# A fused attention and MLP kernel: a changed prologue (homes for x tiles, tile 5's transpose, the order of late loads, V by head group, statistics of tile 3)

## The chip, the cores and the metric

One core of a Trainium2 chip runs the kernel. TensorE (PE in the profile) does matmuls, VectorE (DVE), ScalarE (ACT) and GpSimd (POOL) work elementwise, and SyncE (SP) issues every DMA, in one queue. The metric is the device time of one execution in microseconds; the median of three runs is given.

## The reference

A layer norm of x feeds both an attention block and an MLP; the result gates and is added to x. 2048 rows, 1024 columns, 32 heads of 32, hidden width 3584, bf16.

```python
xn = layernorm(x)
q, k, v = heads(xn @ wqkv)                     # 32 heads of 32
s = (softmax(q @ k.T * 32**-0.5) @ v) @ wo     # over 2048 keys
y = layernorm(xn)
b = gelu(y @ w1 + b1) @ w2 + b2                # 1024 -> 3584 -> 1024
out = x + s * silu(b)
```

## The kernel before, in words

The work is cut in 16 tiles of 128 rows of x. A tile is loaded, its mean and variance are taken, it is normalised to bf16 (`normalize`, line 748) and transposed ("turned") into `xnT`, so that the 1024 columns lie on the partitions. Tiles 0 to 3 are turned on TensorE (`tr_item`, 726) and copied from PSUM by ScalarE (737); tiles 4 to 15 are turned by a DMA (752). The statistics of tile 1 come from two ScalarE passes with accumulators (769); all others from VectorE's two `bn_stats` passes and an aggregate (785, 787). The inverse root is a power on GpSimd (794).

From the turned tiles come the queries and keys of head group 0 in blocks of 256 rows (two tiles): `q_item` and `k_item` (706, 716). VectorE copies queries out of PSUM (712), ScalarE copies keys (722). "K2" below is the keys of tiles 4 and 5. `v_item` (677) makes the values of two head groups at once, two tiles at a time, with a right operand of 256 columns.

Eight head groups of four heads follow one another. For a head group and a block of 256 queries, a *unit* takes 256 keys: one step of eight matmuls writes scores to four of six PSUM banks (line 846), and two ScalarE exponentials of 1024 columns (855) turn them into probabilities. Then matmuls with V (612) accumulate the outputs in one of two further banks, and sums of probabilities come from VectorE adds (`tree`, `tree1`; 872, 886, 1209) and a matmul with ones. In the first head group the order of units is written out by hand (`order0`, 1123): two query blocks run side by side, so that keys are used as they come, and a third is mixed in. There are 504 such units and eight of half width at the end.

The MLP (`w1_item`, `w2_item`), the projections of the following head groups (`proj`) and the output projection fill TensorE between the scores. Weights stream through rings of buffers.

Nothing of this order is decided on the chip. `_Plan` holds all operations with assumed costs, priorities and dependences, and runs a list schedule when the program is built: it fixes the order of each engine's instructions, and puts semaphore waits where an operation needs another engine's result. Each engine then runs its list in order. TensorE work sits in queues named `tr`, `pro`, `q0`, `v0`, `proj`, `mlp`, `w2`, `wo`; an item has a position, a due unit, and `hold`, the unit before which it may not start. Where TensorE would be idle early, the plan inserts dummy matmuls with the identity ("fillers", 668).

x tiles share ten buffers inside `hT`, so tiles 10 to 15 are loaded when an earlier tile is normalised (782). `wv` is loaded right after tile 9.

Of the kernel before, what the change touches and what calls it, by code (L numbers as in the profile page):

```python
# [32 lines left out]
class _Plan:  # L33
# [59 lines left out]
    def run(self):  # L93
# [152 lines left out]
        def pe_step(t):  # L246
# [214 lines left out]
def bass_recurrent_scan__mha_block__mixer_channel_mlp__prompt_kernel(  # L461
# [17 lines left out]
    EPS = 1e-5  # L479
# [13 lines left out]
    with ExitStack() as st:  # L493
# [125 lines left out]

        XS = lambda t: ("xst", t % NXS)  # L620

# [3 lines left out]
        def load_x(t, extra=()):  # L625
            dma(f"x{t}", lambda e: e.dma_start(xst[t % NXS], x2[t * 128:(t + 1) * 128, :]), 262144, [], [XS(t)],
                rate=390.0, prio=2, occ=500, lat=2450, extra=extra)
# [9 lines left out]

        def load_v(pr):
            src = A_wqkv[:, 2 * D + pr * 256: 2 * D + (pr + 1) * 256].rearrange("(c p) n -> p c n", p=128)
            dma("wv", lambda e: e.dma_start(wv[:], src), 524288, [], [("wv",)], prio=2, rate=200.0)  # L640

# [35 lines left out]
        def v_item(pr, n, kind, pos=0.0):  # L677
# [14 lines left out]
            return it  # L692

        def qk_item(hg, which, tq, wi, pos):
            it = _Item("proj", pos)
            sl = hg % 2
            for dc in range(DC):
                def fn(e, b, dc=dc):
                    return mm(e, bank(b), wqk[wi][:, dc, :], xnT[:, dc, tq * 512:(tq + 1) * 512], dc == 0, dc == DC - 1)
                chunk(it, fn, Q512, [("xnT", 4 * tq + k, dc) for k in range(4)] + [("wqk", wi)])  # L700
            nm = "Q" if which == 0 else "K"
            dve(lambda e: e.tensor_copy(QKT[sl][:, which, tq * 512:(tq + 1) * 512], bank(it.bank)), c_ps(512), [],  # L702
                [(nm, sl, 2 * tq), (nm, sl, 2 * tq + 1)], 0, it)
            return it
# [11 lines left out]
        def k_item(n):  # L716
            it = _Item("pro", 0.01 * n)
            for dc in range(DC):
                def fn(e, b, dc=dc):
                    return mm(e, bank(b, 0, 256), wqk[wk0][:, dc, :], xnT[:, dc, n * 256:(n + 1) * 256], dc == 0, dc == DC - 1)  # L720
                chunk(it, fn, Q256, [("xnT", 2 * n, dc), ("xnT", 2 * n + 1, dc), ("wqk", wk0)])
            act(lambda e: e.activation(QKT[0][:, 1, n * 256:(n + 1) * 256], bank(it.bank, 0, 256), ACT.Copy), c_act(256), [],
                [("K", 0, n)], -1, it)
            return it

        def tr_item(t):
            it = _Item("pro", t - 10.0)
            it.bank = [2, 3, 4, 5][t]
            tk = ("S", it.bank // 2, it.bank % 2)

# [16 lines left out]
        def normalize(t, rs):  # L747
            first[t] = dve(lambda e: e.tensor_scalar(xnb[t % 4], xst[t % NXS], mv[:, t, 0:1], lnp[:, t, 1:2],  # L748
                                          op0=ALU.subtract, op1=ALU.mult), c_b4(1024) + 118,
                [XS(t), ("mv", t), rs], [("xnb", t % 4)], 1)  # L750
# [12 lines left out]

        for n in range(NPR):
            groups = [(2 * n,), (2 * n + 1,)] if n < 2 else [(2 * n, 2 * n + 1)]
            for ts in groups:
                if ts == (AT,):
                    for k, f, sc in ((0, ACT.Copy, 1.0 / D), (1, ACT.Square, D ** -0.5)):
                        act(lambda e, k=k, f=f, sc=sc: e.activation(
                            fl3(PA[0])[:, k * 1024:(k + 1) * 1024], xst[AT], f, scale=sc, accum_out=mv[:, AT, k:k + 1]),  # L770
                            c_acts(1024) + 93, [XS(AT)], [("st", AT, k)], 1)
                    dve(lambda e: e.tensor_tensor(lnp[:, AT:AT + 1, 2], mv[:, AT:AT + 1, 0], mv[:, AT:AT + 1, 0], op=ALU.mult), 65,
                        [("st", AT, 0)], [("s2",)], 0.95)
                    dve(lambda e: e.scalar_tensor_tensor(lnp[:, AT:AT + 1, 0], mv[:, AT:AT + 1, 1], EPS, lnp[:, AT:AT + 1, 2], op0=ALU.add,
                                                         op1=ALU.subtract), 65,
                        [("st", AT, 1), ("s2",)], [("ve", AT)], 0.95)
                    dve(lambda e: e.tensor_tensor(mv[:, AT:AT + 1, 1], mv[:, AT:AT + 1, 1], lnp[:, AT:AT + 1, 2], op=ALU.subtract), 65,
                        [("st", AT, 1), ("s2",)], [("mv", AT)], 1.1)
                for t in ts:
                    if t == AT:  # L780
                        continue
                    if t >= NXS:
                        load_x(t, [first[2 * n - 5]])
                    for c in range(2):
                        dve(lambda e, t=t, c=c: e.bn_stats(stats[:, t, c, :], xst[t % NXS][:, c * 512:(c + 1) * 512]),  # L785
                            605, [XS(t)], [("st", t, c)], 1.2)
# [3 lines left out]
                rs = ("rs", lo)  # L790
                if ts != (AT,):
                    dve(lambda e, lo=lo, hi=hi: e.tensor_scalar_add(lnp[:, lo:hi, 0], mv[:, lo:hi, 1], EPS), 80,
# [5 lines left out]
            if n < NTR // 2:  # L798
                plan.dense["tr"] += [tr_item(2 * n), tr_item(2 * n + 1)]
            if n < NG0:  # L800
                pro_q.append(q_item(n))
            pro_q.append(k_item(n))
            pro_q.sort(key=lambda it: it.pos)
# [12 lines left out]
        pool(lambda e: e.tensor_tensor(lnp[:, :, 2], mv[:, :, 1], lnp[:, :, 1], op=ALU.mult), 250,  # L816
             rss + [("mv", t) for t in range(NT)], [("s2",)], 2)
        pool(lambda e: e.tensor_tensor(lnp[:, :, 2], lnp[:, :, 2], lnp[:, :, 1], op=ALU.mult), 250, [("s2",)], [("s2",)], 2)
# [146 lines left out]
        def proj(hg, w):  # L965
            wk = load_qk(hg, 1, [first[9]] if hg == 1 else ())
            wq = load_qk(hg, 0)
# [4 lines left out]
            if hg % 2 == 0:  # L972
                lst += [(8 + 5 * n, "v", n) for n in range(NPR)]
            for pos, kind, t in sorted(lst):
                pos += 64 * w
                if kind == "v":
                    it = v_item(hg // 2, t, "proj", pos)
# [142 lines left out]


        pvs = [_Item("pv") for _ in range(NG0)]
        order0 = [(0, 0), (0, 1), (1, 0), (1, 1), (0, 2), (1, 2), (2, 0), (2, 1)]
# [75 lines left out]
        def tree1(g, us):  # L1199
            pr, tok = PR[g % 2], ("PR", g % 2)  # L1200
            for k in range(4):
# [5 lines left out]
                for m in range(2):  # L1207
                    pi = us[2 * k + m][2]
                    dve(lambda e, d=d, m=m, pi=pi: e.tensor_tensor(d[:, m], Pt[pi][:, :, 0, :], Pt[pi][:, :, 1, :], op=ALU.add),
                        c_b16(1024), [("P", pi, h) for h in range(2)], [dt], 3.2, None, [first[NT - 1]])  # L1210
                if k:
                    dve(lambda e, d=d: e.tensor_tensor(fl3(pr), fl3(pr), fl3(d), op=ALU.add), c_b16(2048), [dt, tok], [tok], 3.2)

# [252 lines left out]
```

## Time and profile before

| | us |
|---|---|
| median of three runs (1034.75 to 1036.66) | 1036.16 |
| the profiled execution | 1036.81 |
| its span, first to last instruction | 1035.0 |
| ScalarE busy in it | 1015.9 |
| TensorE busy | 994.5 |
| VectorE busy | 955.7 |

The profile is of one execution. Busy time is the union of an engine's instructions; the end of a matmul is modelled, so a busy TensorE is not TensorE at its peak. A row of the timeline has the start in the span, the length, engine, line, operation, output and input with shapes and a count, and in brackets the idle time of the engine just before and what ended it. The granted TensorE clock was 0.997 over the span. Lines in rows of before are lines of the kernel before.

### The profile page before, as it was taken

How to read it: one execution, taken by the hardware profiler on the slowest of the kernel's cores; microseconds unless marked ns; L12 is line 12 of the kernel's file. 1: busy time of each engine (PE TensorE's matmuls, PEld its weight loads, DVE VectorE, ACT ScalarE, POOL GpSimd, SP SyncE). 2: the span in 40 equal slices, each digit the busy share in tenths (PEclk: the TensorE clock that was granted, in tenths of full speed). 3: DMA queues.
4: the chain of work that ended last, by engine and by line, in shares of the span. 5: the costliest groups of instructions: out<-in, count | busy, mean ns of one | idle time of the engine just before them, and what ended most of it. 6: DMA issues, size and time to landing. Idle time of an engine off the chain costs nothing.

```text
span 1035.0 us, 31625 instructions
## 1 busy us (share of the span) xinstructions
PE 994.5 (96%) x14148; PEld 633.3 (61%) x14217; DVE 955.7 (92%) x1343; ACT 1015.9 (98%) x1093; POOL 12.2 (1%) x21
## 2 busy tenths in 40 slices
PE   8999999999999999999999999999999999999996
PEld 6656566666766566666665666666656665654433
DVE  7899999899799999997899999998999889978896
ACT  7999999999999999999999999999999999999996
POOL 2200000000000000000000000000000000000000
PEclk9999999999999999999999999999999999999998
DMA  7967756545766657446457575565365762963321
GB/s 204 171 155 212 192 151 188 166 114 153 205 182 143 177 163 221 120 133 190 136 147 196 149 224 164 149 181 160 84 165 161 208 177 70 294 209 121 121 84 53
DMA packets 318199, 167.99 MB, mean 162 GB/s; under 512 B 56688, under 2 KB 306032, under 8 KB 318064
## 3 DMA queue, kind: packets, MB, share of 16 engines
q1 hardware_dynamic: 318064, 165.98, 58.1%
q8 instruction: 111, 1.82, 0.7%
q14 instruction: 24, 0.20, 0.1%
HBM read 146.55 MB, written 12.06 MB: 153 GB/s over the span
## 4 chain that ended last, share of the span: by engine, by line
ACT 84%; PE 9%; DMA 3%; DVE 2%; issue 0%; SPq 0%; POOL 0%; DVEq 0%; another core or an unknown queue 0%
ACT P L855 78%; PE ps L617 6%; ACT ut L1040 4%; DMA w2r<-in_B_w_dram 2%; PE ps L846 2%; PE ps L612 1%; ACT gw L1067 1%; ACT P L1157 1%; DVE stats L785 1%; DMA xnT<-gw 0%; DMA hT<-in_A_x_dram 0%; DVE gw L748 0%; DVE PA L872 0%; DVE hT L1391 0%; ACT w2r L855 0%
## 5 line engine op out<-in xcount | busy, mean ns | idle before, releaser
L855 ACT ACTIVATE P<-ps 128x1024 bf16<-128x1024 f32 x988 | 923.6, 1238 | 2.9 <-PE ps L846 2.8
L872 DVE TENSOR_TENSOR PA<-P 128x2048 bf16<-128x2048 bf16 x173 | 209.5, 1215 | 33.5 <-ACT P L855 32.4
L617 PE MATMUL ps<-yT,w1r 128*128 128x256 bf16 x1792 | 228.2, 273 | 0.8 <-DVE QKT L702 0.5
L617 PE MATMUL ps<-w2r,hT 128*128 128x256 bf16 x1792 | 223.7, 273 | 4.0 <-DMA w2r<-in_B_w_dram 2.6
L846 PE MATMUL ps<-QKT 32*128 32x256 bf16 x4032 | 200.2, 273 | 12.9 <-ACT P L855 9.3
L886 DVE TENSOR_TENSOR PR<-PR,PA 128x2048 bf16<-128x2048 bf16 x173 | 209.4, 1211 | 1.3
L617 PEld LDWEIGHTS ps<-yT,w1r 128*128 128x128 bf16 x1792 | 163.6, 98 | 54.8 <-issue 30.2
L617 PEld LDWEIGHTS ps<-w2r,hT 128*128 128x128 bf16 x1792 | 163.3, 98 | 54.6 <-issue 30.8
L846 PEld LDWEIGHTS ps<-QKT 32*128 32x128 bf16 x4032 | 59.8, 92 | 142.1 <-ACT P L855 135.3
L612 PE MATMUL ps<-P,V 128*32 128x256 bf16 (+1 forms) x4080 | 136.8, 272 | 0.3 <-issue 0.3
L617 PE MATMUL ps<-xnT,wqk 128*128 128x512 bf16 (+1 forms) x507 | 118.7, 360 | 7.2 <-issue 2.0
L612 PEld LDWEIGHTS ps<-P,V 128*32 128x32 bf16 x4080 | 95.8, 96 | 31.3 <-issue 22.5
L617 PE MATMUL ps<-wv,xnT 128*128 128x256 bf16 (+1 forms) x575 | 85.8, 285 | 0.9 <-DVE QKT L702 0.7
L617 PEld LDWEIGHTS ps<-xnT,wqk 128*128 128x128 bf16 x560 | 49.3, 98 | 53.7 <-issue 15.6
L1023 DVE TENSOR_TENSOR hT<-ps,b1T 128x512 bf16<-128x512 f32 x112 | 76.4, 682 | 1.8 <-PE ps L617 1.1
L872 DVE TENSOR_TENSOR PR<-P 128x2048 bf16<-128x2048 bf16 x60 | 72.6, 1210 | 1.0 <-ACT P L855 0.8
L617 PEld LDWEIGHTS ps<-wv,xnT 128*128 128x128 bf16 x576 | 53.0, 98 | 22.2 <-issue 9.3
L1040 ACT ACTIVATE ut<-ut 128x2048 bf16<-128x2048 bf16 (+1 forms) x33 | 62.1, 1883 | 0.0
L941 DVE STREAM_TRANSPOSE nt<-ps 128x256 f32<-128x256 f32 x63 | 27.8, 442 | 14.9 <-PE ps L612 14.8
L702 DVE CAST QKT<-ps 128x512 bf16<-128x512 f32 x58 | 39.6, 683 | 1.8 <-PE ps L617 1.4
L1037 DVE TENSOR_TENSOR ut<-hT 128x2048 bf16<-128x2048 bf16 (+1 forms) x33 | 34.7, 1052 | 0.1
L1042 DVE TENSOR_TENSOR hT<-ut,hT 128x2048 bf16<-128x2048 bf16 (+1 forms) x33 | 34.6, 1050 | 0.0
(107 smaller groups left out, 581.3 us busy)
## 6 DMA issues: line engine op xcount, KB each, us to landing
w1r<-in_B_w_dram SPq DMA_DIRECT2D x112, 512.0 KB, 4.5
w2r<-in_B_w_dram SPq DMA_DIRECT2D x128, 448.0 KB, 4.6
hT<-in_A_x_dram SPq DMA_DIRECT2D x20, 256.0 KB, 3.8
wqk<-in_A_wqkv_dram SPq DMA_DIRECT2D x16, 256.0 KB, 4.3
yst<-in_A_x_dram SPq DMA_DIRECT2D x16, 256.0 KB, 4.7
g_scratch<-gw SPq DMA_DIRECT2D x32, 128.0 KB, 3.8
o_scratch<-ot SPq DMA_DIRECT2D x56, 64.0 KB, 3.6
xnT<-o_scratch SPq DMA_DIRECT2D x7, 512.0 KB, 7.2
```

What stands on the lines that cost most here:

```text
L612: ins = e.matmul(dst(j), lhsT=lhsT(j), rhs=rhs(j), start=start, stop=stop, tile_position=(0, 32 * j), skip_group_check=True)
L617: return e.matmul(dst, lhsT=lhsT, rhs=rhs, start=start, stop=stop, skip_group_check=True)
L702: dve(lambda e: e.tensor_copy(QKT[sl][:, which, tq * 512:(tq + 1) * 512], bank(it.bank)), c_ps(512), [], [(nm, sl, 2 * tq), (nm, sl, 2 * t ...
L846: ins = e.matmul(bank(b0[j], kk * 256, (kk + 1) * 256), lhsT=QKT[sl][32 * j:32 * j + 32, 1, kb * 128:(kb + 1) * 128], rhs=QKT[sl][32 * j:3 ...
L855: x = act(lambda e, h=h: e.activation(Pt[pi][:, 2 * h:2 * h + 2].rearrange("p j k q -> p (j k q)"), ps[:, pr[h] * 1024:(pr[h] + 1) * 1024] ...
L872: return dve(lambda e: e.tensor_tensor(dst[:].rearrange("p u j q -> p (u j) q"), src[:].rearrange("p u j k q -> p (u j) k q")[:, :, 0, :], ...
L886: return dve(lambda e: e.tensor_tensor(fl3(pr), fl3(pr), fl3(PA[i]), op=ALU.add), c_b16(2048), [("PA", i), tok], [tok], 3.2)
L941: dve(lambda e: e.transpose(nt_t[:], bank(pv.bank, 256, 512)), c_ps(256) + 120, [], [("nt",)], prio, pv)
L1023: w1_ev[p] = dve(lambda e: e.tensor_tensor(hT[:, hs], bank(it.bank).rearrange("p (k t) -> p k t", k=2), b1T[:, 2 * pi:2 * pi + 2].unsqueez ...
L1037: dve(lambda e: e.tensor_tensor(u_, x_, x_, op=ALU.mult), c_b16(n), hs_, [("ut", ui)], gp)
L1040: act(lambda e: e.activation(u_, u_, ACT.Tanh, scale=GC), c_acts(n), [("ut", ui)], [("ut", ui)], ga)
L1042: dve(lambda e: e.tensor_tensor(x_, u_, x_, op=ALU.mult), c_b16(n), [("ut", ui)] + hs_, hs_, gp)
```

## The change

- Sixteen homes for the sixteen x tiles: ten in `hT` as before, four in the buffers `PR` (later used for sums of probabilities) and two in `yst` (the MLP's input tiles). A tile's load no longer waits for a buffer. Tiles 10 and 11 are issued directly behind tile 9; tiles 12 to 15 wait for the normalisation of tile 4, and `wv` is issued between tiles 13 and 14, instead of directly behind tile 9.
- Tile 5 is turned on TensorE and copied by ScalarE. The plan may put a waiting transpose between the matmuls of an open item.
- The statistics of tile 3, like those of tile 1, are taken by ScalarE.
- The first queries and keys (tiles 0 and 1) become one item, `qk_first`: 128 columns per matmul, tile 0 first, then tile 1 in two halves. K1 is likewise done tile by tile.
- Keys 3 to 7 of head group 0 are copied by VectorE instead of ScalarE.
- V of head group 0 is made by four items of four tiles with 128 columns (`v_half`); V of head group 1 the same way, later, among the projections.
- The adds of `tree1` get priority 2.3 instead of 3.2 (lower goes first), and the plan assumes longer landing times for the DMA turns of tiles 4, 6 and 7.

```diff
+            tq, th = self.dense["tr"], heads["tr"]
+            if use is None and S["do"] is not None and th < len(tq) and tq[th].chunks[0].left == 0 and tq[th].chunks[0].ready <= t:
+                heads["tr"] += 1
+                tq[th].k = 1
+                S["mode"] = "d"
+                commit(tq[th].chunks[0], t)
+                return
...
-        NTR, NWARM, NG0, AT = 4, 8, 3, 1
+        TRP = (5,)
+        PN = ()
+        NTR, NWARM, NG0, AT = 4, 8, 3, (1, 3)
...
+        for i in range(2):
+            pr_flat = PR[i][:].rearrange("p u j q -> p (u j q)")
+            xst += [pr_flat[:, 0:1024], pr_flat[:, 1024:2048]]
+        xst += [yst_t[i][:] for i in range(2)]
...
-        for t in range(4, NXS):
+        for t in range(NTR, 12):
             load_x(t)
-        load_v(0)
...
+        def v_half(h, m, kind, pos=0.0):
+            it = _Item(kind, pos)
+            for t4 in range(4):
+                for dc in range(DC):
+                    def fn(e, b, t4=t4, dc=dc):
+                        tb = 4 * m + t4
+                        return mm(e, bank(b, t4 * 128, (t4 + 1) * 128), xnT[:, dc, tb * 128:tb * 128 + 128],
+                                  wv[:, dc, h * 128:(h + 1) * 128], dc == 0 and t4 == 0, dc == DC - 1)
+                    chunk(it, fn, Q128, [("xnT", 4 * m + t4, dc), ("wv",)])
+            a = V_SLOTS[0][h]
+            dve(lambda e: e.tensor_copy(V[:, a, 4 * m:4 * m + 4, :], bank(it.bank).rearrange("p (t n) -> p t n", t=4)),
+                c_ps(512), [], [("V", a, 2 * m), ("V", a, 2 * m + 1)], 0, it)
             return it
...
         def k_item(n):
             it = _Item("pro", 0.01 * n)
-            for dc in range(DC):
-                def fn(e, b, dc=dc):
-                    return mm(e, bank(b, 0, 256), wqk[wk0][:, dc, :], xnT[:, dc, n * 256:(n + 1) * 256], dc == 0, dc == DC - 1)
-                chunk(it, fn, Q256, [("xnT", 2 * n, dc), ("xnT", 2 * n + 1, dc), ("wqk", wk0)])
+            for lo, w in ((0, 128), (128, 128)) if n < 2 else ((0, 256),):
+                for dc in range(DC):
...
+            if n >= 3:
+                dve(lambda e: e.tensor_copy(QKT[0][:, 1, n * 256:(n + 1) * 256], bank(it.bank, 0, 256)), c_ps(256), [],
+                    [("K", 0, n)], -1, it)
+                return it
...
+        def qk_first():
+            it = _Item("pro", -0.001)
+            for lo, d0, d1 in ((0, 0, 8), (128, 0, 4), (128, 4, 8)):
+                for k, wi in ((0, wq0), (1, wk0)):
...
         def tr_item(t):
-            it = _Item("pro", t - 10.0)
-            it.bank = [2, 3, 4, 5][t]
+            it = _Item("pro", t - 10.0 if t < NTR else 0.019 + 0.0001 * t)
...
-            if t >= NTR:
+            if t >= NTR and t not in TRP:
                 dma(f"tr{t}", lambda e: e.dma_start_transpose(xnT[:, :, t * 128:(t + 1) * 128], xnb[t % 4]), 262144,
-                    [("xnb", t % 4)], [("xnT", t, c) for c in range(DC)], prio=0, rate=300.0, occ=1300, lat=1000)
+                    [("xnb", t % 4)], [("xnT", t, c) for c in range(DC)], prio=0, rate=300.0, occ=1300, lat={4: 2800, 6: 2400, 7: 2000}.get(t, 1000))
...
         for n in range(NPR):
+            if n == 6:
+                for t in range(12, NT):
+                    load_x(t, [first[4]])
+                    if t == 13:
+                        load_v(0, [first[4]])
...
-                if ts == (AT,):
+                if ts[0] in AT:
...
-                    if t >= NXS:
-                        load_x(t, [first[2 * n - 5]])
...
+            pro_q += [tr_item(t) for t in (2 * n, 2 * n + 1) if t in TRP]
+            if n == 0:
+                pro_q.append(qk_first())
...
-        for n in range(NPR):
-            plan.dense["v0"].append(v_item(0, n, "pro", 0.2 + 0.01 * n))
-            plan.dense["v0"][-1].hold = 6 + 1 * n
+        for n in range(NPR // 2):
+            plan.dense["v0"].append(v_half(0, n, "pro", 0.2 + 0.01 * n))
+            plan.dense["v0"][-1].hold = 6 + 2 * n
...
-            wk = load_qk(hg, 1, [first[9]] if hg == 1 else ())
+            wk = load_qk(hg, 1, [first[NT - 1]] if hg == 1 else ())
...
+            if hg == 1:
+                lst += [(8 + 10 * n, "v1", n) for n in range(NPR // 2)]
...
-                    [("yst", t2)], rate=390.0, extra=[first[11]] if c == 0 else [w1_ev[4]] if c == 1 else ())
+                    [("yst", t2)], rate=390.0, extra=[w1_ev[4]] if c == 1 else ())
...
-                        c_b16(1024), [("P", pi, h) for h in range(2)], [dt], 3.2, None, [first[NT - 1]])
+                        c_b16(1024), [("P", pi, h) for h in range(2)], [dt], 2.3, None, [first[NT - 1]])
```

More of the change, by code (lines that the diff above doesn't have):

```diff
@@ L724, in k_item, with fn @@
             return it
-        def tr_item(t):
-            it = _Item("pro", t - 10.0)
-            it.bank = [2, 3, 4, 5][t]
-            tk = ("S", it.bank // 2, it.bank % 2)
+        def qk_first():
+            it = _Item("pro", -0.001)
+            for lo, d0, d1 in ((0, 0, 8), (128, 0, 4), (128, 4, 8)):
+                for k, wi in ((0, wq0), (1, wk0)):
+                    for dc in range(d0, d1):
+                        def fn(e, b, dc=dc, lo=lo, k=k, wi=wi):
+                            return mm(e, bank(k or b, lo, lo + 128), wqk[wi][:, dc, :], xnT[:, dc, lo:lo + 128],
+                                      dc == 0 and lo == 0, dc == DC - 1)
+                        chunk(it, fn, Q128, [("xnT", lo // 128, dc), ("wqk", wi)], [("S", 0, 1)] if k else ())
+            dve(lambda e: e.tensor_copy(QKT[0][:, 0, 0:256], bank(it.bank, 0, 256)), c_ps(256), [], [("Q", 0, 0)], 0, it)
+            act(lambda e: e.activation(QKT[0][:, 1, 0:256], bank(1, 0, 256), ACT.Copy), c_act(256), [("S", 0, 1)], [("K", 0, 0)], -1)
+            return it
+        def tr_item(t):
+            it = _Item("pro", t - 10.0 if t < NTR else 0.019 + 0.0001 * t)
+            tk = ("ps", t)
+            if t < NTR:
+                it.bank = [2, 3, 4, 5][t]
+                tk = ("S", it.bank // 2, it.bank % 2)
             def fn(e, b):
@@ L790, in bass_recurrent_scan__mha_block__mixer_channel_mlp__prompt_kernel @@
                 rs = ("rs", lo)
-                if ts != (AT,):
+                if ts[0] not in AT:
                     dve(lambda e, lo=lo, hi=hi: e.tensor_scalar_add(lnp[:, lo:hi, 0], mv[:, lo:hi, 1], EPS), 80,
@@ L1119, in mlp @@
                 (mq if s_[0] == "w1" else plan.dense["w2"]).append(it)
+        for i in range(2):
+            after([("PR", i)], [XS(10 + 2 * i), XS(11 + 2 * i)])
+            after([("yst", i)], [XS(14 + i)])
         pvs = [_Item("pv") for _ in range(NG0)]
```

61 lines of the change are left out of this document (36 added, 25 removed).

## The prediction

> **What bounds the kernel now.** I read the page's totals first, then the engines by stretch, then ScalarE's instructions in the opening, then what these wait for.
>
> ```profile
> PE 994.5 (96%) x14148; PEld 633.3 (61%) x14217; DVE 955.7 (92%) x1343; ACT 1015.9 (98%) x1093; POOL 12.2 (1%) x21
> ```
>
> ScalarE (ACT) is the bound: all but 19.1 of the span's 1035.0 us are its work. The engines by stretch (length, then busy time of each) say where the 19.1 us are:
>
> ```profile
> 0.00:24.00 24.00, 19.86 (x265) 16.47 (x265) 18.77 (x51) 16.40 (x23) 5.51 (x13) 1.00 0.74 210
> 24.00:60.00 36.00, 33.31 (x521) 23.08 (x523) 32.22 (x62) 35.23 (x42) 6.67 (x8) 1.00 0.97 185
> 60.00:1024.00 964.00, 938.63 (x13242) 591.90 (x13312) 898.21 (x1220) 962.62 (x1029) 0.00 (x0) 1.00 0.58 162
> 1024.00:1035.00 11.00, 2.69 (x129) 1.88 (x129) 6.55 (x14) 1.67 (x3) 0.00 (x0) 0.71 0.15 49
> ```
>
> ScalarE is the fourth engine: idle for 7.60, 0.77, 1.38 and 9.33 us. The change edits the first stretch and what feeds the second. So its worth is how much earlier the same exponential runs, plus ScalarE work taken away after that. ScalarE in the opening (start, length, line):
>
> ```profile
> 7.31 1.02 ACT L737 ACTIVATE xnT<-ps 128x1024 bf16<-128x1024 bf16 x1 [0.81 <-PE ps L733]
> 9.05 2.07 ACT L737 ACTIVATE xnT<-ps 128x512 bf16<-128x512 bf16 x3 [0.71 <-PE ps L733]
> 11.85 0.38 ACT L722 ACTIVATE QKT<-ps 128x256 bf16<-128x256 f32 x1 [0.72 <-PE ps L617]
> 12.73 1.02 ACT L855 ACTIVATE P<-ps 128x1024 bf16<-128x1024 f32 x1 [0.51 <-PE ps L846]
> 13.65 1.02 ACT L737 ACTIVATE xnT<-ps 128x1024 bf16<-128x1024 bf16 x1
> 14.56 1.03 ACT L855 ACTIVATE P<-ps 128x1024 bf16<-128x1024 f32 x1
> 15.81 0.38 ACT L722 ACTIVATE QKT<-ps 128x256 bf16<-128x256 f32 x1 [0.22 <-PE ps L617]
> 16.70 4.69 ACT L855 ACTIVATE P<-ps 128x1024 bf16<-128x1024 f32 x5 [0.51 <-PE ps L846]
> 22.68 0.38 ACT L722 ACTIVATE QKT<-ps 128x256 bf16<-128x256 f32 x1 [1.28 <-PE ps L617]
> 22.96 1.94 ACT L855 ACTIVATE P<-ps 128x1024 bf16<-128x1024 f32 x2
> ```
>
> Exponentials are numbered e0, e1 ... Here e0 runs at 12.73, e2 at 16.70, e7 at 22.96 and, 0.92 later, e8 at 23.88. The long gap is before the copy of K2 (keys of tiles 4 and 5) at 22.68: its matmuls waited for tile 5's turn by DMA. The normalisation of tiles 4 and 5 on VectorE, TensorE's 128-column fillers (early and late) and the wait for the DMA turn, and two answers on DMA issues by line (median us to landing last):
>
> ```profile
> 15.11 1.00 DVE L748 TENSOR_SCALAR gw<-hT,mv,lnp 128x1024 bf16<-128x1024 bf16 x2 [0.23 <-POOL lnp L794]
> ```
> ```profile
> 2.20 3.92 PE L668 MATMUL ps<-ident 128*128 128x128 bf16 x47
> ...
> 13.07 1.61 PE L668 MATMUL ps<-ident 128*128 128x128 bf16 x26
> ...
> 21.59 1.70 PE L617 MATMUL ps<-xnT,wqk 128*128 128x256 bf16 x14 [1.43 <-DMA xnT<-gw]
> ```
> ```profile
> xnT<-gw SPq DMA_TRANSPOSE x1, 2.9
> ...
> xnT<-gw SPq DMA_TRANSPOSE x1, 6.3
> ```
>
> These two are issue-to-landing times of tile 4's turn (issued 15.69, queue empty) and tile 8's (29.82, behind four loads of x); tile 5's took 4.5.
>
> **The change, part by part.** Order from the changed program, durations from the rows above and their neighbours.
>
> *Tile 3's statistics on ScalarE.* Two passes at 1.06 (as tile 1's from 4.31) and an accumulator read: +2.1 us on ScalarE, and VectorE loses two statistics passes (0.61 each in a row), the 0.21 aggregate and one add for three tiny operations. Tile 3 lands at 7.02 (issued 2.1, 4.9 to land), so the first pass runs 7.05 to 8.1, and the copy of turned tile 0, queued behind it, moves from 7.31 to 8.1. On VectorE the first tiny operation for tile 3 waits for that pass, until 8.25, where before it went on at 7.72; behind it stand tile 2's add, its power on GpSimd (0.55 to 0.78), the normalisations of tiles 1 (8.4) and 2 (9.25, was 8.85), and TensorE's turns of them. The second pass runs 9.0 to 10.1, so turned tile 1 is copied in halves at 10.05 and 10.55 (was 9.05), turned tile 2 at 11.05 to 12.0.
>
> *Queries and keys 0 by tile.* Sixteen 128-column matmuls for tile 0 run from 9.3, when the query weights land (3.4 + 5.9), until 10.4, beside the waits for tile 1; sixteen for tile 1 end at 12.0 (62 ns each, 1.61/26). VectorE copies Q0 after a statistics pass, 12.45 to 12.85, scores end at 13.3. Tile 3 is normalised 11.45 to 12.0 (was 11.31), turned by 12.65, and its copy now stands ahead of e0: 12.65 to 13.6. So e0 is at 13.57, later than 12.73, but that copy is done. K1's copy follows, e1 at 14.8, e2 at 15.7: 1.0 ahead of 16.70.
>
> *Tile 5 on TensorE.* Tiles 4 and 5 are normalised 14.75 to 15.7 (was 15.11 to 16.1). TensorE turns 5 by 16.35 (0.46 plus latency); its copy costs ScalarE 0.92 after e2, at 16.6. Then e3 to e7 run 17.5 to 22.1. Tile 4's turn is issued at 15.3 with nothing queued ahead, so it lands between 18.0 (2.7, the shortest) and 21.6 (6.3); nearest is its own old row, 2.9, or 4.5 as tile 5's, 18.2 to 19.8. K2's matmuls follow the scores at 20.35 and end at 21.3; the copy waits for e7, 22.1; its scores take 22.5 to 22.9 and e8 starts at 22.95. Against 23.88 that is 0.93 gained. A landing at 21.6 would cost 0.5 of it.
>
> *Copies of K3 to K7 to VectorE.* Five copies leave saturated ScalarE; each holds it for 0.26 to 0.28 (48.93 to 49.19 at the next exponential): 1.33 gained. VectorE gets five of 0.38; it idled 3.8 us between 24 and 60.
>
> *V by head group.* 16 x 8 matmuls of 256 columns for two groups become 128 of 128 columns now and 128 later. In the eleven intervals between scores that hold them (the seventh to the seventeenth), TensorE has 1.73 us each (62 ns for 128 columns, 114 for 256, 0.33 for scores) against 1.83 for two exponentials; before, scores were 2.04 apart from 24.95 to 53.53 (fourteen intervals), waits included. Bounds for a 128-column V matmul: 57 ns (half of 114) to 83 (3.92/47); I take 62, the warm row. The Trainium skill, page "TensorE: Matmul & The Clock Gate", section "Back-to-back issue gap", gives about 81 ns sustained at 128 columns, by which the sum would be 1.3 us longer (19 ns x 128, less 1.1 of spare time in those intervals); the trace has 62, and the same section's 131 ns at 512 columns does not fit this trace (0.23 us each at 64.84). The second half runs after the twenty-second scores, where an interval with 16 such holds 1.56 us.
>
> *Loads.* Own homes let tiles 10 and 11 load at 9.2, in wv's old place; tiles 12 to 15 and wv (1.5 MB) are issued 16.6 to 19, behind tile 4's turn. On SP the turn of tile 6 comes next, at 21.2, when the tile is normalised (was 20.8 for the normalisation). wv: 5.5 (median) to 7.0 (in the opening) from 17.5, so 23.0 to 24.5; needed at 24.25 behind e8's scores: no more than 0.2 lost. Turn 7, issued 22.6, lands 25.4 to 28.9; K3 is wanted at 26.6 with 0.5 spare: nothing lost up to 27.1, 1.5 to 1.8 at the worst; I take 4.5 (27.1), so nothing.
>
> *VectorE after that.* With these rows it reaches the first V copy at 27.85 and the second at 32.0, so the third V item starts 0.3 late, and 0.1 more follows: 0.4 idle to 60, against 0.77. The tree adds of lower rank and the late y loads hide behind ScalarE's exponentials; without that cover a wait of 0.3 to 0.9 (the longest for a weight load) would show. Beyond 60 the instructions are of the same kinds and numbers, but for the late V; the last 215 exponentials and all that stands beside them come in the same order, so the tail's 9.33 stays. In the reordered middle the bounds are 0.74 gained (its idle at 150 to 180) and 1.5 lost (two such places); I take 0, as its TensorE intervals stay at or below those before.
>
> Sum: 0.93 + 1.33 + 0.37 = 2.6 us. The profiled execution took 1036.81 (span 1035.0 and 1.81 around it), so 1034.2; that execution is 0.65 above the median 1036.16, so the median to expect is **1033.6**.
>
> **The rivals.**
> *A. The middle gains too.* No idle left from 24 to 60 and none in 150 to 180: 0.4 + 0.74 more, 1032.5. For it: 1.73 against 1.83. Against: VectorE's late V copies.
> *B. Turns 6 and 7 come late* behind the 1.5 MB: like tile 8's 6.3 and tile 9's 6.0. K3's matmuls end at 29.5, e14 at 29.95 instead of 28.45: 1.5 lost, 1035.1. It decides from a landing after 27.1.
> *C. 128-column V matmuls cost 83 ns:* 128 x 21 = 2.7 us more in intervals with 11 x 0.10 = 1.1 spare: 1.6 lost, 1035.2. Speaking for it: the 47 fillers; against: 62 in three later rows. The Trainium skill's 81 ns, named above, lies just short of it.
> *D. Slower: ScalarE bounds the opening.* Statistics (2.1), tile 5's copy (0.92) and the wait for tile 3 ahead of tile 0's copy (0.8) all push e8, and the 1.28 us gap before K2 stays: 3.9 - 1.33 = 2.6 lost, 1038.8. It decides if e2 starts after 16.7. Against it: VectorE's statistics head the path from 5.4 to 16.
>
> **How the numbers follow.** Forecast 0.50, own range 1032.6 to 1034.9; A 0.17, B 0.11, C 0.09, D 0.13. A measurement tells about 0.2% (2.07 us) from no change, so faster is below 1034.09: A and 0.36 of the forecast, 0.53. Within: 0.14 of it, B and C, 0.34. Slower, above 1038.2: D, 0.13. The range 1031.9 to 1037.0 takes in all but D and some tails.
>
> **What would show it.** Right: e0 near 13.6, e2 near 15.7, e8 near 23, no 1.28 us gap before K2's copy, three key copies on ScalarE, under 0.6 idle from 24 to 60, busy ScalarE 1017.6 (+2.1 + 0.92 - 1.33). Wrong: e2 after 16.7 (D); a wait of the third to sixth keys for a DMA turn (B); TensorE rows of V above 75 ns (C); new idle in the middle, which no row of before can exclude.

## The result, and the profile after

The changed kernel takes 1032.22 us (median of 6 runs, 1030.78 to 1034.5) beside 1036.78 for the kernel before in the same comparison (6 runs): a ratio of 0.9961, 95% interval [0.9949, 0.9974]. The same kernel timed once more gave 0.998 [0.9971, 0.999] (1033.34, 8 runs, beside 1035.39, 26 runs). The two intervals only just overlap, so a ratio can move from one comparison to the next by about the width of its interval. Weighted by their intervals the two make 0.9973, which is 2.8 us faster (by its ratio 4.0 in the first, where the medians above differ by 4.6, and 2.1 in the second). The forecast was 1033.6, 2.6 faster. So the number held. The experiments below say how much of it is what the prediction reasoned about.

The profiled execution of the changed kernel has a span of 1030.3 us (before: 1035.0). Its totals, and its engines by stretch:

```profile
PE 1004.7 (98%) x14355; PEld 636.6 (62%) x14355; DVE 956.3 (93%) x1347; ACT 1016.9 (99%) x1093; POOL 11.8 (1%) x21
```
```profile
0.00:24.00 24.00, 19.52 (x283) 16.15 (x283) 19.57 (x55) 20.13 (x29) 5.50 (x13) 1.00 0.93 235
24.00:60.00 36.00, 34.36 (x584) 22.70 (x581) 32.37 (x66) 34.27 (x38) 6.28 (x8) 0.95 0.91 168
60.00:1020.00 960.00, 947.51 (x13364) 595.72 (x13364) 897.28 (x1214) 959.97 (x1026) 0.00 (x0) 1.00 0.58 162
1020.00:1031.00 11.00, 3.29 (x133) 2.04 (x132) 7.10 (x14) 2.54 (x4) 0.00 (x0) 0.89 0.20 70
```

ScalarE (the fourth engine) is still the bound. It idles 3.87 us in the first stretch where it idled 7.60, and 1.73 in the second where it idled 0.77, at a granted clock of 0.95 there. In the long middle it idles 0.03 instead of 1.38, and at the end about 7.8 instead of 9.3. The last two were forecast not to change. ScalarE in the opening (start, length, line, and in brackets its idle time just before):

```profile
11.57 0.40 ACT L768 ACTIVATE QKT<-ps 128x256 bf16<-128x256 f32 x1
12.29 1.02 ACT L784 ACTIVATE xnT<-ps 128x1024 bf16<-128x1024 bf16 x1 [0.32 <-PE ps L780]
13.21 1.02 ACT L911 ACTIVATE P<-ps 128x1024 bf16<-128x1024 f32 x1
14.12 0.39 ACT L754 ACTIVATE QKT<-ps 128x256 bf16<-128x256 f32 x1
14.38 1.96 ACT L911 ACTIVATE P<-ps 128x1024 bf16<-128x1024 f32 x2
16.19 1.07 ACT L784 ACTIVATE xnT<-ps 128x1024 bf16<-128x1024 bf16 x1
17.09 4.75 ACT L911 ACTIVATE P<-ps 128x1024 bf16<-128x1024 f32 x5
21.61 0.51 ACT L754 ACTIVATE QKT<-ps 128x256 bf16<-128x256 f32 x1
22.62 3.77 ACT L911 ACTIVATE P<-ps 128x1024 bf16<-128x1024 f32 x4 [0.51 <-PE ps L902]
27.46 1.94 ACT L911 ACTIVATE V<-ps 128x1024 bf16<-128x1024 f32 x2 [1.06 <-PE ps L902]
```

e0 runs at 13.21, e2 at 15.34, e8 at 22.62. Nothing but the copy of tile 3 (12.29), of K1 (14.12), of tile 5 (16.19) and of K2 (21.61) stands between the exponentials. The 1.28 us gap before K2's copy is gone. What is left is the 0.51 before e8 and, new, 1.06 at 27.46. TensorE around that gap:

```profile
19.83 1.91 PE L630 MATMUL ps<-xnT,wqk 128*128 128x256 bf16 x16
...
24.45 2.41 PE L630 MATMUL ps<-wv,xnT 128*128 128x128 bf16 x25 [0.35 <-DMA wv<-in_A_wqkv_dram]
26.79 0.61 PE L902 MATMUL ps<-QKT 32*128 32x256 bf16 x8
```

K2's sixteen matmuls waited for no transfer (tile 4's turn was in time). V's first 25 matmuls waited 0.35 us for `wv` and then took 96 ns each, not 62, and the scores behind them 0.61 instead of 0.40. The engines by stretch say why (the number after POOL's count is the granted clock):

```profile
20.00:24.00 4.00, 2.77 (x36) 1.78 (x34) 4.00 (x12) 3.50 (x6) 0.70 (x1) 1.00 1.65 285
24.00:25.00 1.00, 0.65 (x14) 0.55 (x11) 1.00 (x3) 1.00 (x2) 0.00 (x0) 0.99 0.06 23
25.00:28.00 3.00, 3.00 (x34) 2.39 (x32) 1.81 (x5) 1.94 (x3) 0.70 (x1) 0.50 0.98 220
28.00:29.00 1.00, 1.00 (x11) 0.84 (x8) 0.69 (x1) 1.00 (x2) 0.00 (x0) 0.81 0.89 204
```

Half the clock, from about 25.0 to 28.4, after four microseconds in which TensorE was busy for 2.77.

### The profile page after: what moved, and what is told of

Same layout as the page of the kernel before. It is cut to its first block, busy times and chain, and to the rows that moved or that the text cites. A ratio compares the mean times of both kernels' runs of the same rounds, so it can differ in the third digit from the quotient of the medians.

```text
span 1030.3 us, 31971 instructions
## 1 busy us (share of the span) xinstructions
PE 1004.7 (98%) x14355; PEld 636.6 (62%) x14355; DVE 956.3 (93%) x1347; ACT 1016.9 (99%) x1093; POOL 11.8 (1%) x21
## 3 DMA queue, kind: packets, MB, share of 16 engines
q8 instruction: 112, 1.84, 0.7%
## 4 chain that ended last, share of the span: by engine, by line
ACT 84%; PE 7%; DVE 5%; DMA 2%; issue 0%; SPq 0%; POOL 0%; DVEq 0%
ACT P L911 78%; PE ps L630 4%; ACT ut L1101 4%; PE ps L625 2%; ACT gw L1128 1%; PE ps L902 1%; ACT P L1221 1%; DVE PA L928 1%; DMA wv<-in_A_wqkv_dram 1%; DVE stats L837 1%; DVE PR L942 1%; DVE hT L1084 1%; DMA yst<-in_A_x_dram 1%; DVE gw L796 0%; DMA hT<-in_A_x_dram 0%; DMA xnT<-gw 0%
## 5 line engine op out<-in xcount | busy, mean ns | idle before, releaser
L630 PE MATMUL ps<-xnT,wqk 128*128 128x512 bf16 (+2 forms) x584 | 131.3, 354 | 1.1 <-DVE nv L1010 0.3
L625 PEld LDWEIGHTS ps<-P,V 128*32 128x32 bf16 x4080 | 95.6, 96 | 32.7 <-issue 22.6
L630 PE MATMUL ps<-wv,xnT 128*128 128x256 bf16 (+2 forms) x704 | 89.7, 267 | 1.6 <-DMA xnT<-gw 0.6
L630 PEld LDWEIGHTS ps<-wv,xnT 128*128 128x128 bf16 x704 | 56.5, 99 | 25.6 <-issue 11.6
```

The source lines that it names most:

```text
L625: ins = e.matmul(dst(j), lhsT=lhsT(j), rhs=rhs(j), start=start, stop=stop, tile_position=(0, 32 * j), skip_group_check=True)
L630: return e.matmul(dst, lhsT=lhsT, rhs=rhs, start=start, stop=stop, skip_group_check=True)
```

## The experiments

Five terms read from each profile carry the comparison: ScalarE's idle time to 24 us, its work in the whole span, its idle time from 24 to 60, from 60 to 1010, and from there to the end. Their sum is the span. "Near" is the sum of the first three, which is all that the forecast changed. In us, against the profile of the kernel before, but for the seed pair, which is against that kernel with the same seed:

| | idle to 24 | work | 24–60 | near | middle | end | span |
|---|---|---|---|---|---|---|---|
| forecast | -3.95 | +1.7 | -0.37 | -2.6 | 0 | 0 | -2.6 |
| changed | -3.73 | +1.0 | +0.96 | -1.8 | -1.35 | -1.57 | -4.7 |
| changed, once more | -3.79 | +1.5 | -0.06 | -2.4 | -0.24 | -1.59 | -4.2 |
| changed, seed 0 | -4.30 | +1.1 | +0.58 | -2.6 | -2.19 | -1.37 | -6.2 |
| before + 16 fillers | +0.33 | +0.56 | -0.43 | +0.5 | -1.38 | -1.59 | -2.5 |

(The forecast's idle time to 24 is its e8, 0.93 earlier with 3.02 more work ahead of it.) One profile is one execution. The times are medians with intervals.

**A clock kept up** (twenty identity matmuls ahead of the sixth scores, where the changed kernel has four):
```diff
+            if n == 2:
+                warm2 = _Item("pro", 0.0235)
+                for _ in range(5):
+                    chunk(warm2, lambda e, b: filler(e, b, 4), 240, [("xnT", 4, 0)])
+                pro_q.append(warm2)
```


> The changed kernel with sixteen more identity matmuls on TensorE between the fifth and sixth scores (20 in place of 4). In the changed kernel's profile the granted clock falls to 0.50 from 25.0 to 28.2, right after four thin microseconds of TensorE, and ScalarE then idles 1.06 us before an exponential. Theory, the thin stretch takes the clock down: here the clock stays at 1.00, the 25 V matmuls take 1.6 us and not 2.4, the 1.06 us are gone, and the kernel is 1.0 us faster than the changed one (ratio to before about 0.995). Rival, the late wv (a wait of 0.35) is what costs: the gap stays above 0.7 us and the time within 0.3 us of the changed kernel.

Ratio 0.9975 [0.9965, 0.9984]. The clock stayed at 1.00 and ScalarE idled 0.96 from 24 to 60, so the 1.06 us gap went; the longest there is now 0.72, before the exponential behind K3's matmuls, which waited 0.84 for tile 7's turn. But the clock also stayed up without these fillers. This is the unaltered changed kernel, once more:

> The changed kernel unaltered, once more. Its first profile had the granted clock at 0.50 from 25.0 to 28.2 and 1.73 us of ScalarE idle time from 24 to 60, while the kernel with the keys back on ScalarE, with the same TensorE order up to there, had 1.00 and 0.58. Theory, the dip depends on where an execution falls in the gate's own time and not on the order alone: here it may be absent, and then the idle time from 24 to 60 is 0.4 to 1.0 and the span about 1029.5. Rival, the dip belongs to this order: it is there again, with a gap of about 1 us. Ratio to before 0.995 to 0.998; tail after the last exponential 8.4 us if that goes with the program, 9.7 to 9.9 possible if it varies by execution.

```profile
20.00:24.00 4.00, 2.77 (x38) 1.87 (x35) 4.00 (x12) 3.50 (x6) 0.70 (x1) 1.00 1.43 292
24.00:25.00 1.00, 1.00 (x24) 0.87 (x17) 1.00 (x3) 1.00 (x2) 0.00 (x0) 1.00 0.17 41
25.00:28.00 3.00, 2.50 (x36) 1.74 (x33) 2.50 (x6) 3.00 (x4) 0.70 (x1) 1.00 1.10 247
```
```profile
24.14 1.57 PE L630 MATMUL ps<-wv,xnT 128*128 128x128 bf16 x25
...
27.02 1.05 PE L630 MATMUL ps<-xnT,wqk 128*128 128x256 bf16 x8 [0.50 <-DMA xnT<-gw]
...
42.79 0.45 PE L630 MATMUL ps<-wv,xnT 128*128 128x128 bf16 x5 [0.58 <-DMA xnT<-gw]
```

The same 2.77 us of TensorE in the same four, and no dip: whether the clock falls here differs from one execution to the next. Nor does the wait for `wv`, which this execution lacks, decide it: the kernel with ScalarE's key copies (below) has the same 2.77, a wait of 0.32 for `wv` behind it, and no dip. V's matmuls take 62 ns, and K3 waits 0.50 for its turn, which the dip had hidden. The last row is V's wait for the turn of tile 15; ScalarE's longest idle time from 24 to 60 follows it (0.40 at 43.62). The fillers' effect on the median is not shown.

**Tile 3's statistics back on VectorE:**
```diff
-        NTR, NWARM, NG0, AT = 4, 8, 3, (1, 3)
+        NTR, NWARM, NG0, AT = 4, 8, 3, (1,)
...
```


> The changed kernel with tile 3's statistics back on VectorE. Theory of the prediction, VectorE's statistics head the opening's path: e2 starts later than the changed kernel's 15.3, by 0.5 to 1.0, and the time rises by 0.5 to 1.0 us although ScalarE has 2.1 us less to do. Rival D, ScalarE bounds the opening: e2 and e8 start earlier, and the time falls by up to 1.3 us.

Ratio 0.999 [0.9982, 0.9999], 1.8 us slower than the changed kernel taken at 0.9973. In its timeline of ScalarE, e2 and e8 are 1.0 later than in the changed kernel, while ScalarE has 1.7 us less to do:

```profile
16.30 1.02 ACT L911 ACTIVATE P<-ps 128x1024 bf16<-128x1024 f32 x1 [0.50 <-PE ps L902]
...
23.61 3.77 ACT L911 ACTIVATE P<-ps 128x1024 bf16<-128x1024 f32 x4 [0.51 <-PE ps L902]
```

So VectorE's statistics head the opening, and D had the wrong engine.

**Tile 5 turned by DMA again:**
```diff
-        TRP = (5,)
+        TRP = ()
```


> The changed kernel with tile 5 turned by DMA again. Theory: the copy of K2 waits for that turn as before; issued at about 16.3 and landing 2.9 to 4.5 later, e7 ends 0.9 earlier (no copy of tile 5), and e8 starts between 22.3 and 23.2, so between 0.3 us faster and 0.6 us slower than the changed kernel. Rival: the turn on TensorE is the main part of the gain, e8 goes back to about 23.9 and the time rises by 1.2 us or more.

Ratio 1.0021 [1.001, 1.0033], 4.9 us slower than the changed kernel taken at 0.9973. My theory was too small, and the rival's price (1.2 or more) held for another reason than its e8 near 23.9: e8 is at 23.41, only 0.8 late. The rest is in ScalarE's and TensorE's timelines:

```profile
35.13 1.02 ACT L911 ACTIVATE P<-ps 128x1024 bf16<-128x1024 f32 x1 [4.28 <-PE ps L902]
```
```profile
30.89 1.05 PE L630 MATMUL ps<-xnT,wqk 128*128 128x256 bf16 x8 [1.84 <-DMA xnT<-gw]
32.88 1.44 PE L630 MATMUL ps<-xnT,wqk 128*128 128x256 bf16 x6 [0.94 <-DMA xnT<-gw]
```

K3 and K4 wait for the turns of tiles 6 to 9. With one turn more in the queue ahead of 1.5 MB of loads, the turns of tiles 6 and 7 were issued only from 21.9 and came behind those loads. This is rival B's mechanism, in a kernel where it decides. The waits are not all of it: behind the first of them the granted clock is 0.50 from 32.0 to 38.8, so the scores ahead of the exponential at 35.13 take 0.61 instead of 0.40, and the key matmuls are slowed alike.

**Keys 3 to 7 copied by ScalarE again:**
```diff
-            if n >= 3:
+            if n >= 99:
```


> The changed kernel with the copies of K3 to K7 back on ScalarE. Theory: five copies of 0.27 us on a saturated ScalarE, so 1.33 us slower than the changed kernel (ratio to before about 0.9975). Rival: these copies stood in gaps that ScalarE has anyway in that stretch (1.73 us from 24 to 60), so the time stays within 0.4 us of the changed kernel.

Ratio 0.9974 [0.9961, 0.9987], not told apart from the changed kernel. In the profile ScalarE works 1.0 us longer than in the changed kernel once more, and near is 0.9 worse (0.3 worse than in the first profile, which had the clock dip). A copy (32.93) still puts off the next exponential (33.19) by 0.26, so the price in the prediction holds in the rows. In the time its effect is within the scatter.

**V by pairs of groups, as before:**
```diff
-        for n in range(NPR // 2):
-            plan.dense["v0"].append(v_half(0, n, "pro", 0.2 + 0.01 * n))
-            plan.dense["v0"][-1].hold = 6 + 2 * n
+        for n in range(NPR):
+            plan.dense["v0"].append(v_item(0, n, "pro", 0.2 + 0.01 * n))
+            plan.dense["v0"][-1].hold = 6 + 1 * n
...
-            if hg == 1:
+            if hg == 99:
```


> The changed kernel with V made for two head groups at once, 256 columns per matmul, all in the opening. Theory, relief of TensorE: from 24 to 54 TensorE has V of both groups again, scores are about 2.0 us apart as before, ScalarE's idle time from 24 to 60 rises to 1.5 to 3 us, and the kernel is 0.5 to 1.5 us slower than the changed one. Rival C, 128-column matmuls cost more than half of a 256-column one: undoing them gains up to 1 us.

Ratio 0.9989 [0.9978, 0.9999]. ScalarE idles 2.33 from 24 to 60, 2.2 of it at 58.48 for TensorE, which itself had waited 1.6 for VectorE's V copy at 55.73 and then had the clock at 0.50 from 57.4 to 60.8 (40 matmuls with V took 2.36 there, and 1.28 at full clock with the loads back). The time is 0.9 us above that of the unaltered kernel in the same comparison, about the expected 1 us, though the two intervals overlap. And 128 columns at 62 ns cost nothing: C falls.

**The loads at their old times** (own homes kept):
```diff
-        for t in range(NTR, 12):
+        for t in range(NTR, 10):
             load_x(t)
+        load_v(0)
...
-            if n == 6:
-                for t in range(12, NT):
-                    load_x(t, [first[4]])
-                    if t == 13:
-                        load_v(0, [first[4]])
...
+                    if t >= 10:
+                        load_x(t, [first[2 * n - 5]])
```


> The changed kernel with its own homes for the x tiles kept, but the loads at their old times: wv right behind tile 9, tiles 10 to 15 when an earlier tile has been normalised. Theory of the prediction, the new times of the loads are worth little by themselves: e8 within 0.4 of 22.6, wv lands before it is wanted (no wait for it), the turns of tiles 8 to 11 stand behind loads again, and the time is within 0.7 us of the changed kernel. Rival, the late loads are a main part of the gain because they free the turns: K3 or K4 wait for a turn, 1.5 us or more slower.

Ratio 1.0035 [1.0022, 1.0048]: 5.5 us slower than the unaltered kernel in the same comparison. My theory was wrong. The rival had the size (1.5 us or more), but not the place: the turns of tiles 6 and 7 take 3.0 and 2.9 here, and K3 and K4 wait for none. TensorE's timeline, and ScalarE's:

```profile
42.50 0.51 PE L630 MATMUL ps<-wv,xnT 128*128 128x128 bf16 x6 [2.51 <-DMA xnT<-gw]
...
46.70 3.74 PE L630 MATMUL ps<-xnT,wqk 128*128 128x256 bf16 x16
```
```profile
50.85 1.94 ACT L909 ACTIVATE w1r<-ps 128x1024 bf16<-128x1024 f32 x2 [3.69 <-PE ps L900]
```

Tile 14 is loaded only at 30.4, and VectorE waits 1.11 for it (at 34.30) before it goes on to normalise tiles 12 and 13, at 35.5 and 36.3. Their turns are issued from 36.1, the second takes 5.1, and V's matmuls of tile 13 wait 2.51 for it. ScalarE, now further on, needs these tiles earlier than the kernel before did. Then the clock halves: it is 0.50 from 43.6 to 50.5, and the sixteen matmuls at 46.70 take 3.74 where K2's sixteen took 1.91 (19.83 in the changed kernel). By the rows of that stretch (0.61 + 1.89 + 3.74 against 0.40 + 1.07 + 1.91 at full clock) I estimate 2.9 us of the loss to be the clock. The mean granted clock is 0.993 to 0.995 in all five executions, against 0.997 to 0.999 in the fourteen of the changed kernel, so the fall is not the profiled execution's alone. Without the earlier loads the change ends slower than the kernel before.

**The kernel before with another order** (the planner's third random seed at zero), and **the changed kernel with the same seed:**
```diff
-        0, 0, 234914347, 0,
+        0, 0, 0, 0,
```


> The kernel before, with the one nonzero seed of its plan (stretch 60 to 90 us) set to zero: nothing changes up to 60 us, and the order after that differs. This is the size of order luck alone. Theory, 1.4 us of middle and 1.6 us of tail in the measured gain are not made by any part of the change: here the opening is as before (e8 at 23.9), the middle's idle time is anywhere from 0.0 to 2.5 us, the tail 8.4 or 9.8, and the time within 0.2% of before. Rival, middle and tail were good because of the change: here they stay at 1.4 and 9.9 (each within 0.3).

> The changed kernel with the third random seed of the planner at zero, as in the run of the kernel before with that seed (1037.2, ratio 1.0023). If the change's 2.8 us are what the opening gains, this kernel is 2.8 us faster than that one too: ratio 0.9994 to 1.0000, with the opening as in the changed kernel (e8 at 22.7). If they are a good draw of the middle's order and the tail, it has lost them: ratio 1.0015 or more.

The kernel before: 1.0023 [1.0014, 1.0032], with 2.19 idle in the middle instead of 1.38. The changed one: 0.9962 [0.995, 0.9974]. So with this seed the change gains 0.61%, 6.3 us, over two comparisons. Near gives 2.6 of the 6.2 between the profiles, as forecast. The other 3.6 are again middle and end.

**K2's copy on VectorE too**, and **the same with `wv` ahead of tiles 12 and 13:**
```diff
-            if n >= 3:
+            if n >= 2:
...
+                load_v(0, [first[4]])
                 for t in range(12, NT):
                     load_x(t, [first[4]])
-                    if t == 13:
-                        load_v(0, [first[4]])
```


> The changed kernel with K2's copy on VectorE too. My theory: in the changed kernel that copy is held on ScalarE until the exponential before it ends, and costs its own 0.27 and the 0.51 gap until the scores that need it are done; on VectorE the chain is done while ScalarE still has exponentials, so the exponential that was at 22.7 runs at about 21.9 and the time is 0.7 us shorter, a ratio near 0.9966 where the unaltered one has 0.9974 over its two measurements. Rival: VectorE, 97% full there, waits for K2's matmuls with the statistics of tiles 8 and 9 behind it, so turns 6 and 7 are late and the gain goes: more idle from 24 to 60, the time the same or up to 1 us longer.

> As the run before, and wv is issued ahead of tiles 12 and 13 instead of behind them. My theory: V's matmuls, which waited 0.35 us for wv, wait for nothing, so another 0.3 us of ScalarE's idle time from 24 to 60 goes; tiles 12 and 13 land 1.3 us later and are not missed. Rival: with exponentials 0.7 earlier and turns 6 and 7 behind the same bytes, K3 is what TensorE waits for, and wv's place is worth nothing: within 0.3 us of the run before.

Ratios 0.9972 [0.9963, 0.9981] and 0.9967 [0.9956, 0.9979]. In the first, e8 runs at 21.41, 1.2 earlier than in the changed kernel. Of this, 0.46 is there at e0 already (12.75 instead of 13.21: tile 3 landed earlier); the other 0.75 is the edit's, where 0.7 was expected. Yet the time is that of the changed kernel. The profiled execution was the fastest of twelve, 2.1 us below their median, so it can't say what the others lost; but its end shows one loss (TensorE, among the last small matmuls):

```profile
1020.59 0.28 PE L625 MATMUL ps<-P,ones 128*32 128x128 bf16 x7
1021.85 0.33 PE L625 MATMUL ps<-P,ones 128*32 128x128 bf16 x9 [0.98 <-issue]
```

"Issue" is time in which the engine waited for nothing that the profile shows. The second has such a stop of 0.71 there, and e8 at 22.06, as far behind its e0 as in the first. Its idle time from 24 to 60 is 1.66, against 1.24 in the first, so the 0.3 us expected from the earlier `wv` did not come. None of these versions is shown to beat the changed kernel.

**The kernel before with 16 more fillers at its very start:** `NWARM` at 24 instead of 8, at an unchanged assumed cost, so that the order is the same on every engine.
```diff
-        NTR, NWARM, NG0, AT = 4, 8, 3, 1
+        NTR, NWARM, NG0, AT = 4, 24, 3, 1
...
-        chunk(warm, warm_fn, 110.0 * NWARM, [("ident",)], [("S", 0, 0)])
+        chunk(warm, warm_fn, 110.0 * 8, [("ident",)], [("S", 0, 0)])
```


> The kernel before with 16 more identity matmuls at its very start, in the order of TensorE and nowhere else: every later TensorE instruction lies 16 matmuls further along its stream. The first turn waits for a normalised tile until 6.65 and the fillers end at 6.1, so at most 0.5 us is lost at the start. If the 1.2 us in which TensorE stops among the last small matmuls hangs on where those stand in the instruction stream, the stop moves by 16 matmuls or goes, and without it the tail is 8.4 from the last full exponential instead of 9.9: ratio near 0.999. If it belongs to the kernel's way of ending, it stays at the same matmul, and the ratio is 1.000 to 1.0005.

Ratio 0.9976 [0.9966, 0.9986]: 2.4 us faster, more than either reading expected, by sixteen dummy matmuls, in a profile whose opening is 0.35 later (e8 at 24.23; with seed 0, which leaves the opening alone, e8 was at 24.07, so about half of this is within the scatter). Its engines by stretch:

```profile
0.00:24.00 24.00, 20.39 (x280) 17.33 (x281) 18.66 (x50) 16.07 (x22) 5.52 (x13) 1.00 0.78 205
24.00:60.00 36.00, 33.96 (x524) 23.23 (x525) 32.49 (x63) 35.66 (x44) 6.57 (x8) 1.00 0.97 189
60.00:1020.00 960.00, 936.13 (x13208) 590.79 (x13273) 896.05 (x1213) 960.00 (x1025) 0.00 (x0) 1.00 0.58 162
```

ScalarE idles not at all in the middle. TensorE's timeline shows the two things that went, first in the kernel before, then in this one:

```profile
175.42 0.72 PE L617 MATMUL ps<-w2r,hT 128*128 128x256 bf16 x5 [0.92 <-DMA w2r<-in_B_w_dram]
...
916.97 0.28 PE L617 MATMUL ps<-w2r,hT 128*128 128x256 bf16 x1 [0.70 <-DMA w2r<-in_B_w_dram]
...
1025.48 0.34 PE L612 MATMUL ps<-P,ones 128*32 128x128 bf16 x12
1027.04 0.24 PE L612 MATMUL ps<-P,ones 128*32 128x128 bf16 x4 [1.21 <-issue]
```
```profile
172.58 2.47 PE L617 MATMUL ps<-w2r,hT 128*128 128x256 bf16 x21
...
1024.57 0.40 PE L612 MATMUL ps<-P,ones 128*32 128x128 bf16 x16
1026.50 0.38 PE L617 MATMUL ps<-yst,xnT 128*128 128x512 bf16 x1 [1.53 <-DVE xnT L1191]
```

The two waits for an MLP weight, and a stop of 1.21 us after twelve of the last sixteen small matmuls, are not there. The changed kernel's profiles lack the stop too, and so do those of its versions with the clock kept up, tile 5 by DMA, ScalarE's key copies, V by pairs and seed 0. The stop is there in both seeds of the kernel before (1.21, 1.17), with tile 3's statistics back (1.17), with the loads back (1.54) and, smaller, in the two with K2's copy on VectorE. ScalarE's idle time in the middle lies anywhere from 0 to 2.2 us, so one profile doesn't tell which of the 1.38 there is the fillers' and which an execution's scatter. The 2.4 us of the medians do say that the fillers bring most of what they seem to. So the 1.35 and 1.57 by which the changed kernel's profile is ahead in the middle and at the end need not be the change's own: a shift of TensorE's instruction stream that computes nothing brought 1.38 and 1.59 in its one profile.

What makes the stop is open. Instructions arrive by DMA in 16 KB pieces (111 of them, 1.82 MB, in the kernel before), and where the stop was (behind 12, 11, 7, 7, 5 or 3 of the last sixteen matmuls), the last piece came one to three microseconds ahead of it (in the kernel before between 1024 and 1025). Of the eight profiles without the stop, six have the last piece within about 0.5 us of these matmuls' end; but the other two have it nearly 3 us ahead of them, and did not stop. The number of matmuls alone doesn't decide either, since two kernels with 14355 of them differ in it. That it hangs on where the instructions stand in the stream rests on this one kernel.

## Why the prediction was right, and where it wasn't

- **The opening's exponentials.** e0, e2, e8 forecast at 13.57, 15.7, 22.95; measured 13.21, 15.34, 22.62 (once more: 13.32, 15.44, 22.73). Each step is 0.2 to 0.4 early from the same place on: tile 3 landed at 6.7, not 7.02, so tiles 4 and 5 were normalised from 14.37 instead of 14.75. The gain at e8 was 1.26, 0.33 more than the term, and that surplus is the luck of this landing, not the change: over seven profiles with this opening e0 lies anywhere from 12.77 to 13.67, and e8 always 9.40 to 9.41 behind it, against 9.38 in the forecast. Putting tile 3's statistics back showed that VectorE's statistics carry it, and D's e2 after 16.7 did not come.
- **K2's copy behind e7** (21.61 against 22.1), its scores' 0.51 behind that, and tile 4's turn in time: as forecast. With the copy on VectorE that 0.51 vanished and e8 came 0.75 closer to e0, so the chain was read rightly.
- **The key copies, 1.33.** The size per copy holds in the rows. Putting them back cost 0.3 to 0.9 in near and nothing that the time can tell.
- **Idle time from 24 to 60, forecast 0.4:** 0.71 once, 1.73 with the clock dip, 1.93 with seed 0. This term was mis-sized, and its place was wrong: I put it at VectorE's V copies, and no row of these profiles shows TensorE waiting for one there. Of the 0.71, 0.40 follows the turn of tile 15, 0.19 stands at 54.92 and 0.12 is K3's wait for the turn of tile 7. That turn took the 4.5 that I took, in both profiles; but the issue of tile 6's turn ahead of it held the queue for 1.68 and 2.45 us (1.35 for tile 4's, with nothing ahead), so in the first profile it was issued at 23.12, not 22.6. K3's wait cost ScalarE 0.12 here and 0.7 in the profiles with seed 0 and with the clock kept up: B's place, at up to half its price. `wv` came 0.35 late in the first profile (forecast: at most 0.2).
- **V in 128 columns:** 62 ns at full clock, the warm row and not the 83 of C.
- **The loads, "nothing lost":** nearly true (K3's 0.1 to 0.7 above, which the old load times don't have). But the working gave them no worth, and undoing them cost 5.5 us. The sub-step that failed is that their cover was never priced: with everything earlier by a microsecond, the old load times of tiles 12 to 15 are what VectorE and then TensorE wait for, and the clock falls behind that wait.
- **The middle, taken as 0, and "the tail's 9.33 stays":** the tail step is wrong. I argued from an unchanged order; the 1.2 us stop in the tail follows no order that I looked at, and it went. The middle came out between -0.24 and -2.19, past the bound of 0.74. Near alone gave -1.8 to -2.6 in three pairs of profiles, two of them with the same profile of before, so the forecast's reasons hold at 70 to 100% of their size.
- **Why the total still agrees: partly luck.** The profiles differ by 4.2 to 4.7, with 1.8 to 2.9 of it in the middle and the end, which the forecast left at 0. The medians of the first comparison differ as much (4.6). Those of the second differ by 2.1: the kernel before had a median of 1035.39 there, 1.4 below its profiled execution, and the repeat's profile lay 0.7 below its own median. So 2.8 is an average of two comparisons that don't agree well. How much of the medians' 2.8 is near and how much is middle and end can't be settled with these runs. Against the kernel before with 16 fillers (0.9976), the changed kernel is between 0.15% faster (0.9961) and no faster (0.998), and with seed 0, in the same comparison, 0.14% faster, each with some 0.15% either way. So these runs don't show that the change beats the kernel before with sixteen dummy matmuls by what the opening gains.

## What to carry to other kernels

Follow the chain that ends last in the stretch that is edited, and price it by rows: that came out within 0.4 us here. Price a moved load by what would wait if it stayed, not only by whether it is late where it went. And before a gain of a few tenths of a per cent is put down to an edit, shift the kernel by something that does nothing (a few dummy instructions, another seed): here that moved the time nearly as much as the whole change. And where an engine is made to wait, look at its clock behind the wait: with the loads back the half clock cost about as much as the wait itself.

## What the hardware showed that I had not expected

- TensorE's clock was halved for 3.4 us in one execution of the changed kernel (0.99, 0.50 for three microseconds, 0.81 of the next: 0.02 + 3 + 0.38) and not in another with the same 2.77 us of work in the four before. The Trainium skill, page "TensorE: Matmul & The Clock Gate", section "What's actually happening", says that activity is judged in free-running windows of about 3.4 us, and that the clock is either full or half. The length and the level agree with this trace. It says that an idle window brings the half clock, but here no stretch of 3.4 us was idle: TensorE was busy 69% of the four microseconds before. Nor was one idle ahead of the three other falls before the tail: after single waits of 2.51 us (loads back), 1.84 (tile 5 by DMA) and 1.61 (V by pairs) the clock was halved for 6.8, 6.8 and 3.4 us, and after waits of 1.43 (the kernel before, 21.59) and 1.58 (tile 5 by DMA, 21.44) it was not.
- TensorE stopped for 0.7 to 1.5 us within a row of independent small matmuls at the end of six profiles out of fourteen, and in eight it didn't. The kernel before has it with two seeds, and lacks it in the one profile with sixteen matmuls more at the start.
- One `wv` of 512 KB and four tiles of x, issued at 16.4 to 19.2, made the next turn, tile 6's, take 6.1 and 5.4 us (the changed kernel and once more) and the one behind it 4.5, against 2.9 for tile 4's with an empty queue; and the issue of tile 6's turn held SP for 2.45 and 1.68 us instead of 1.35. One turn more in that queue cost 4.9 us of the whole, the half clock behind it included.
